# A one-core decode block: the rows of w_out loaded by other queues in other shares, the MLP in 8 pieces instead of 14, x loaded row by row

## The chip, the core and the metric

The kernel runs on one core of one Trainium2 chip. A core has a matrix engine (TensorE; PE in the profile, with its weight loads as PEld), a vector engine (VectorE, DVE), a scalar engine (ScalarE, ACT), a general engine (GpSimd, POOL) and a queue engine that mostly starts transfers (SyncE, SP). Sixteen DMA engines move data between the large memory (HBM) and the on-chip memory (SBUF), whose 128 partitions are called lanes here; matrix products land in PSUM. The metric is the time of one execution in device microseconds (us). Before the change it is 661.87 us, the median of 3 runs (661.77 to 662.01).

## What is computed

One token of each of four sequences (B = 4, D = 640) goes through attention over a cache of 4096 positions with 32 heads of 128, and, beside it, through a gated MLP; both are added to x. Cut to what matters:

```
xn = layernorm(x)                                            # x: 4 x 640
q  = xn @ wq                                                 # wq: 640 x 4096
o  = softmax(q . k_cache / sqrt(128)) . v_cache              # caches: 4 x 32 x 4096 x 128 each
z  = gelu(xn @ w_in)                                         # w_in: 640 x 1728
z1, z2 = z[:, :864], layernorm(z[:, 864:])
g  = w_sp * z2 + b_sp                                        # w_sp, b_sp: one number each
out = x + o @ wo + (z1 * g) @ w_out                          # wo: 4096 x 640, w_out: 864 x 640
```

All tensors are bf16. Nearly all bytes are in the two caches: 128 MiB each, of 282 MB read in all.

## The kernel before, in words

Work goes by units. A unit is 8 heads of one sequence, there are 16 of them (NU), and a unit's K and V are 8 MB each. In SBUF each lane holds 256 consecutive positions of one head, so a load of a unit is 128 lanes by 64 KB, each lane contiguous in HBM. A unit's K is worked on in four quarters (NK = 4); quarters live in a ring of seven places (`ring`). V has one place, `v_all`, of 64 KB a lane.

For each of the 64 quarters (the loop in the `manual_schedule` part) VectorE multiplies the quarter by q (`product`, L537) and adds its halves (`fold_half`, L543), TensorE sums the rest into PSUM (`sums`, L555), and VectorE reduces (`row_sums`, L569). Softmax follows once a unit (L578 to L607), then the products with V on TensorE (`weighted`, L631).

**Loads.** All large loads are issued by SyncE, in the order of the list `loads`. `pump()` goes down that list as long as the places that a load needs are free; a place is freed by the TensorE work that last read it. The list begins: the first quarter of K of unit 0, the second, `load_w` (w_in and those parts of w_out that go in one transfer), the other two quarters, `load_w_few` (the parts of w_out that go in several), K of unit 1, V of unit 0, K of unit 2 and so on. wq is issued ahead of all of them (L118). x, w_sp and b_sp are issued by ScalarE; w_sp and b_sp only inside the scheduled part, behind the first copy of q (L735, L736). A transfer signals its end on one of eight semaphores that transfers share in turn, so its issue can wait for an earlier transfer of the same semaphore.

**Places of the weights.** wq, w_in and the first 640 rows of w_out lie in `v_all` until the MLP is done, the other 224 rows of w_out in `p_buf`, which later holds the softmax weights `p_m`. V of unit 0 can therefore be loaded only once the MLP has read its weights.

**The MLP** (`gmlp`, a generator that the loop advances during the first two quarters) follows the rows of w_out: the hidden features are taken in pieces, and a piece is a set of features that lie on the lanes as the rows of w_out do. `W_OUT` lists parts as (lanes, rows a lane, transfers): 128 lanes of 5 rows, 128 lanes of 1 row, and 12 lanes of 8 rows in 4 transfers of 3 lanes. That makes NFC = 5 + 1 + 8 = 14 pieces. Each piece costs 10 products for z (two halves by five chunks of D, L404) and 2 for the output (L503); the small VectorE operations between work on all pieces at once (L414 to L500).

**The start.** GpSimd makes the identity and some constants; x is normalized on VectorE and ScalarE (L265 to L274), transposed on TensorE (L289), and multiplied by wq (L303) when that has landed.

**The end.** After V of unit 15 comes the last group of wo, in six transfers (L228, L231). The last products with it (L699), a copy (L823) and two small stores (L824, L825) end the program.

Of the kernel before, what the change touches and what calls it, by code (L numbers as in the profile page):

```python
# [10 lines left out]
BF16 = mybir.dt.bfloat16  # L11
# [6 lines left out]
def kernel(  # L18
# [40 lines left out]
    RW = 8  # L59
    QW = HC * Dh  # L60
    RING = 2 * NK - 1
    W_OUT = ((P, 5, 1), (P, 1, 1), (12, 8, 4))
    assert sum(n * r for n, r, _ in W_OUT) == Fh
    NFC = sum(r for _, r, _ in W_OUT)

    def up(n):
        return -(-n // 256) * 256

    PW = sum(up(r * D) for _, r, _ in W_OUT[1:])
    NOH = D // 2  # L70
    CB = 4
    NG = NR // CB
# [8 lines left out]
    const = ctx.enter_context(tc.tile_pool(name="const", bufs=1))  # L81
# [16 lines left out]

    ring = places.tile([P, RING, QW], BF16, name="k_ring")
    x_bf = ring[0:Bsz, 1, 0:D]  # L100
    nc.scalar.dma_start(out=x_bf, in_=A_x.flatten_outer_dims())
    v_all = places.tile([P, NK * QW], BF16, name="v_all")

    wq_sb = v_all[:, 0 : DC * HD].rearrange("p (c n) -> p c n", c=DC)
# [2 lines left out]

    at_v = up(DC * (HD + F))
    w_parts, f0, at_p = [], 0, 0
    for n, r, t in W_OUT:  # L110
        if f0 == 0:
            room = v_all[0:n, at_v : at_v + r * D]
        else:
            room = p_buf[0:n, at_p : at_p + r * D]
            at_p += up(r * D)
        w_parts.append((room.rearrange("p (k n) -> p k n", k=r), f0, n, r, t))
        f0 += n * r
    nc.sync.dma_start(out=wq_sb, in_=A_wq.rearrange("(p c) n -> p c n", c=DC))  # L118

    def load_part(part):  # L120
        w, f0, n, r, t = part
        rows = B_w_out[f0 : f0 + n * r].rearrange("(p k) n -> p k n", k=r)
        for l in range(t):
            nc.sync.dma_start(out=w[l:n:t], in_=rows[l:n:t])

    def load_w():
        nc.sync.dma_start(out=w_in_sb, in_=B_w_in.rearrange("(p c) n -> p c n", c=DC))
        for part in w_parts:
            if part[4] == 1:
                load_part(part)  # L130

    def load_w_few():
        for part in w_parts:
            if part[4] > 1:
                load_part(part)

    w_rows = [
        (w[:, i], f0 + i, n, r) for w, f0, n, r, _ in w_parts for i in range(r)
    ]
# [20 lines left out]
    def k_load(u, r0=0, r1=NK):  # L160
        at = k_at[u][r0:r1]

        def go():
            nc.sync.dma_start(
                out=ring[:, at[0] : at[0] + r1 - r0, :],
                in_=run_of(A_k_cache, u)[:, r0 * QW : r1 * QW].rearrange("p (r w) -> p r w", w=QW),
            )

        return go, at
# [22 lines left out]
    def wo_load(hg):  # L192
        return (lambda: load_wo(hg)), [WO_AT]

    loads = [k_load(0, 0, 1), k_load(0, 1, 2), (load_w, []), k_load(0, 2, 4), (load_w_few, []), k_load(1)]
    for u in range(NU - 4):
        loads += [v_load(u), k_load(u + 2)]
        if u % Bsz == Bsz - 1:
# [65 lines left out]
    for i in range(NSTAT):  # L264
# [5 lines left out]
        out=rstd[:], in_=mv[:, 1:2], func=ACT.Sqrt, bias=eps_tile[:Bsz], scale=1.0  # L270
# [4 lines left out]
        out=xn_bf,  # L275
# [4 lines left out]
        op1=ALU.mult,  # L280
    )

    wsp_bf = const.tile([1, 1], BF16)
    bsp_bf = const.tile([1, 1], BF16)

    xn_v = xn_bf.rearrange("b (p c) -> b c p", c=DC)
    xnT_ps = ps_m.tile([P, DC, Bsz], BF16, tag="m")
    for c in range(DC):
        nc.tensor.transpose(  # L289
            out=xnT_ps[:, c, :], in_=xn_v[:, c, :], identity=ident[:Bsz, :Bsz]  # L290
# [8 lines left out]
    for e in range(PAR):  # L299
        q_ps = ps_pv.tile([P, HG, Dh], FP32, tag="pv", name="q_ps")  # L300
        for c in range(DC):
            for k in range(NQ):
                nc.tensor.matmul(  # L303
                    out=q_ps[k * QD : (k + 1) * QD],
# [15 lines left out]
        out=hot[:].rearrange("p c h -> p (c h)"),  # L320
        in_=ident[:].rearrange("p (g m) -> p m g", m=QD),
# [23 lines left out]
    with nc.allow_low_precision("0 and 1"):  # L345
        nc.vector.tensor_reduce(
            out=own[:],
            in_=ident[:].rearrange("p (h l) -> p h l", h=HT),
# [5 lines left out]
        out=par[:], in_=own[:].rearrange("p (k e) -> p e k", e=PAR), axis=AX.X, op=ALU.add  # L354
# [3 lines left out]
        out=far[:],  # L358
# [13 lines left out]
    for half in range(2):  # L372
        nc.tensor.matmul(
            out=out_ps[OG * half : OG * half + OG, :],
# [16 lines left out]
    for n, r, _ in W_OUT:  # L391
        if by_lanes and by_lanes[-1][0] == n:
            by_lanes[-1] = (n, by_lanes[-1][1] + r)
        else:
            by_lanes.append((n, r))

    def gmlp():
        zz, gw, gt, gz = (gm[n] for n in ("zz", "gw", "gt", "gz"))
        zT = ps_pv.tile([P, 2, NFC, Bsz], FP32, tag="pv", name="zT")
        for t in range(2):  # L400
# [12 lines left out]
        for n, ks in by_lanes:  # L413
# [19 lines left out]

        s_ps = ps_m.tile([1, 2, NFC, Bsz], FP32, tag="m", name="ln_ps")
        nc.tensor.matmul(
# [79 lines left out]
    def stage_q(u):  # L515
        hg, b = divmod(u, Bsz)
        qb_ps = ps_m.tile([P, Dh], FP32, tag="m", name="qbc_ps")
        for e in range(PAR):
            nc.tensor.matmul(  # L519
                out=qb_ps[:],  # L520
                lhsT=of_row[:, e, b].rearrange("p k f l -> p (k f l)"),
                rhs=q_rows[e][:, hg, :],
                start=(e == 0),
                stop=(e == PAR - 1),
            )
        qbcs[u] = small.tile([P, Dh], BF16, name="qbc")
        nc.scalar.copy(out=qbcs[u][:], in_=qb_ps[:])  # L527
# [204 lines left out]
    E = mybir.EngineType  # L732
    with tc.manual_schedule(engines={E.PE, E.DVE, E.Activation, E.SP}):
        stage_q(0)
        nc.scalar.dma_start(out=wsp_bf[:], in_=B_w_sp[0:1, 0:1])  # L735
        nc.scalar.dma_start(out=bsp_bf[:], in_=B_b_sp[0:1].rearrange("(a b) -> a b", a=1))  # L736
        waiting = None
        mlp = gmlp()
        for n in range(NK * NU):
            u, i = divmod(n, NK)  # L740
# [33 lines left out]
            if n in turns:  # L774
                w = waiting = turns[n]
# [19 lines left out]
            out=den[:],  # L795
# [8 lines left out]
        u, b = NU - 1, Bsz - 1  # L804
# [51 lines left out]
```

## Time and profile before

| | before |
|---|---|
| median of 3 runs | 661.87 us (661.77 to 662.01) |
| the profiled execution: its own time | 662.09 us |
| the profiled execution: its span | 660.2 us |
| bytes read from HBM | 282.24 MB, 428 GB/s over the span |
| busy share: DVE, PE, PEld, ACT, POOL | 79%, 48%, 21%, 5%, 2% |
| DMA queue of SP (q1): packets, share of 16 engines | 8192, 99.1% |
| instruction loads (q8, q14): packets | 16 and 4 |
| DVE waiting for K to land (L537) | 87.9 us |

The span runs from the first to the last instruction of the profiled execution; what lies around it, 1.87 us, belongs to the execution's time as well. The page's DMA row gives the busy share of the sixteen DMA engines in 40 slices of the span, and the row below it what they moved. The trace also keeps each DMA packet with its queue, start, duration and bytes: a packet is one lane's contiguous piece, up to 64 KB, and each transfer ends on each DMA engine that serves it with a packet of 4 bytes that raises its semaphore. A packet doesn't name its DMA engine.

### The profile page before, as it was taken

Reading aid. Unit: us, or ns where it says so; the run is one execution under the profiler, and the core shown is the slowest. Engines: PE = TensorE matmul, PEld = TensorE weight load, DVE = VectorE, ACT = ScalarE, POOL = GpSimd, SP = SyncE. Lnnn points to the kernel's source line nnn. Section 1 sums busy time; section 2 is a strip of 40 time slices with the busy share of each in tenths; the row PEclk is TensorE's granted clock in tenths of the full one; section 3 lists DMA queues with packets and bytes.
Section 4 is the critical chain, followed back from the end, with each engine's and each line's share of the span. In section 5 each row is a group of like instructions: output and inputs, shape, how many; then the busy total and the mean of one; then the engine's idle time right before and its main releaser. Section 6 shows DMA issues by size and latency. Waiting matters only on the chain.

```text
span 660.2 us, 4777 instructions
## 1 busy us (share of the span) xinstructions
PE 317.0 (48%) x2083; PEld 136.3 (21%) x2083; DVE 522.6 (79%) x276; ACT 29.9 (5%) x73; POOL 10.1 (2%) x20
## 2 busy tenths in 40 slices
PE   0574372526427363452636336263452534737367
PEld 0231121212213121120212112121120211212124
DVE  1767978959597795969959598695969969999950
ACT  0020000000000000000000000000000000000000
POOL 2300000000000000000000000000000000000000
PEclk9757676766767676585767768676685867676785
DMA  9999999999999999999999999999999999999997
GB/s 369 433 461 434 417 441 434 433 437 438 421 445 426 437 430 441 437 422 433 434 441 441 418 437 441 430 441 421 434 441 437 426 421 445 422 427 436 449 409 284
DMA packets 8232, 282.55 MB, mean 428 GB/s; under 512 B 892, under 2 KB 2184, under 8 KB 2568
## 3 DMA queue, kind: packets, MB, share of 16 engines
q1 hardware_dynamic: 8192, 282.25, 99.1%
q8 instruction: 16, 0.26, 0.1%
q10 hardware_dynamic: 20, 0.01, 0.0%
q14 instruction: 4, 0.03, 0.0%
HBM read 282.24 MB, written 0.01 MB: 428 GB/s over the span
## 4 chain that ended last, share of the span: by engine, by line
DMA 62%; DVE 28%; PE 8%; issue 1%; ACT 0%; DVEq 0%
DMA k_ring<-in_A_k_cache_dram 53%; DVE k_ring L537 14%; DVE k_ring L543 7%; PE s_ps L555 6%; DMA v_all<-in_A_v_cache_dram 4%; DMA k_ring<-in_A_wo_dram 3%; DVE s_sb L569 3%; DMA v_all<-in_A_wq_dram 2%; DVE p_m L607 1%; DVE m L578 1%; PE q_ps L303 1%; PE pv L631 1%; PE out_ps L699 1%; DVE p_m L678 1%; DVE mf L580 1%
## 5 line engine op out<-in xcount | busy, mean ns | idle before, releaser
L537 DVE TENSOR_TENSOR k_ring<-k_ring,qbc 128x8192 bf16<-128x8192 bf16 x64 | 282.9, 4420 | 88.5 <-DMA k_ring<-in_A_k_cache_dram 87.9
L555 PE MATMUL s_ps<-k_ring,ident 128*128 128x512 bf16 x512 | 202.2, 566 | 313.8 <-DVE k_ring L543 313.7
L555 PEld LDWEIGHTS <-ident 128*128 128x128 bf16 x512 | 64.0, 130 | 430.0 <-issue 245.4
L543 DVE TENSOR_TENSOR k_ring<-k_ring 128x4096 bf16<-128x4096 bf16 x64 | 145.9, 2280 | 1.1
L631 PE MATMUL pv<-v_all,p_m 128*32 128x512 bf16 x960 | 62.5, 419 | 0.0
L569 DVE TENSOR_REDUCE s_sb<-s_ps 128x128 f32<-128x1024 f32 x32 | 39.0, 1218 | 3.7 <-PE s_ps L555 3.7
L607 DVE TENSOR_TENSOR p_m<-p_c,own 128x2048 bf16<-128x2048 bf16 x16 | 36.6, 2285 | 0.7 <-ACT p_c L596 0.7
L631 PEld LDWEIGHTS <-p_m 128*32 128x32 bf16 x992 | 26.6, 106 | 42.5 <-issue 23.3
L596 ACT ACTIVATE p_c<-s_sb,nm 128x256 bf16<-128x256 f32 x16 | 8.1, 508 | 342.9 <-DVE nm L588 342.9
L662 PEld LDWEIGHTS o_ps<-o_rows,pick 128*128 128x128 f32 x96 | 20.4, 294 | 4.3 <-issue 3.3
L662 PE MATMUL o_ps<-o_rows,pick 128*128 128x128 f32 x96 | 19.1, 367 | 0.0
L643 ACT COPY o_rows<-pv 128x512 f32<-128x512 f32 x16 | 9.4, 586 | 165.7 <-PE pv L631 165.7
L311 DVE TENSOR_SCALAR q_rows<-q_ps 128x512 bf16<-128x512 f32 x2 | 1.4, 692 | 12.8 <-PE q_ps L303 12.8
L817 DVE TENSOR_TENSOR o_n_last<-o_last,rden_all 128x32 bf16<-128x32 f32 x1 | 0.2, 192 | 12.2 <-PE o_last L809 12.2
L303 PE MATMUL q_ps<-v_all,xnT 128*32 128x512 bf16 x40 | 4.5, 630 | 9.3 <-DMA v_all<-in_A_wq_dram 9.3
L527 ACT CAST qbc<-qbc_ps 128x128 bf16<-128x128 f32 x16 | 4.3, 266 | 97.6 <-PE qbc_ps L519 97.6
L578 DVE TENSOR_REDUCE m<-s_sb 128x1 f32<-128x256 f32 x16 | 6.7, 420 | 0.5
L519 PE MATMUL qbc_ps<-q_rows,of_row 128*128 128x128 bf16 x32 | 6.0, 276 | 0.6 <-DVE q_rows L311 0.6
L519 PEld LDWEIGHTS <-of_row 128*128 128x128 bf16 x32 | 4.1, 132 | 8.1 <-issue 7.4
L716 PE MATMUL o_last<-hot,o_rows 128*128 128x8 f32 x32 | 4.9, 279 | 0.7 <-ACT o_rows L643 0.7
L716 PEld LDWEIGHTS o_last<-hot,o_rows 128*128 128x128 f32 x32 | 4.8, 226 | 1.8 <-ACT o_rows L643 1.6
L699 PE MATMUL out_ps<-k_ring,p_m 128*4 128x320 bf16 x48 | 4.0, 309 | 2.1 <-DVE p_m L691 2.1
(87 smaller groups left out, 81.4 us busy)
## 6 DMA issues: line engine op xcount, KB each, us to landing
k_ring<-in_A_k_cache_dram SPq DMA_DIRECT2D x5, 4096.0 KB, 27.2
v_all<-in_A_v_cache_dram SPq DMA_DIRECT2D x2, 4096.0 KB, 28.2
v_all<-in_A_wq_dram SPq DMA_DIRECT2D x1, 5120.0 KB, 15.4
k_ring<-in_A_k_cache_dram SPq DMA_DIRECT2D x2, 2048.0 KB
k_ring<-in_A_v_cache_dram SPq DMA_DIRECT2D x1, 4096.0 KB
k_ring<-in_A_wo_dram SPq DMA_DIRECT2D x3, 1280.0 KB, 20.6
v_all<-in_B_w_in_dram SPq DMA_DIRECT2D x1, 2160.0 KB
k_ring<-in_A_v_cache_dram SPq DMA_DIRECT2D x1, 2048.0 KB
```

The lines of the kernel that those rows point to most:

```text
L303: nc.tensor.matmul(out=q_ps[k * QD : (k + 1) * QD], lhsT=xnT[:, c, :], rhs=wq_v[:, c, k, e], start=(c == 0), stop=(c == DC - 1),)
L519: nc.tensor.matmul(out=qb_ps[:], lhsT=of_row[:, e, b].rearrange("p k f l -> p (k f l)"), rhs=q_rows[e][:, hg, :], start=(e == 0), stop=(e ...
L537: nc.vector.tensor_tensor(out=t, in0=t, in1=qbcs[u][:, None, :].to_broadcast([P, HC, Dh]), op=ALU.mult)
L543: nc.vector.tensor_tensor(out=t[:, :, 0:HD2], in0=t[:, :, 0:HD2], in1=t[:, :, HD2:Dh], op=ALU.add)
L555: nc.tensor.matmul(out=s, lhsT=ident[:], rhs=t[:, :, g * RW : (g + 1) * RW], start=(g == 0), stop=(g == m - 1),)
L569: nc.vector.tensor_reduce(out=scores[u][:].rearrange("p (r c) -> p r c", r=NK)[:, lo : hi + 1 : hi - lo], in_=sums_ps.pop(n // 2)[:], axis ...
L578: nc.vector.tensor_reduce(out=m1[:], in_=scores[u][:], axis=AX.X, op=ALU.max)
L607: nc.vector.tensor_tensor(out=p_m[:, u % 2], in0=p_c.pop(u)[:].rearrange("p (g c) -> p g c", c=CB)[:, :, :, None].to_broadcast([P, NG, CB, HT]
L631: nc.tensor.matmul(out=pvs[u][cg * QD : (cg + 1) * QD, :], lhsT=p_m[:, u % 2, g0 + n].rearrange("p c h -> p (c h)"), rhs=v_at[:, n * CB : ...
L662: nc.tensor.matmul(out=gr[hg][:], lhsT=pick[:, c, Bsz - 1 - b : P + Bsz - 1 - b], rhs=o[:, c, :], start=(b == 0 and c == 0), stop=(b == Bs ...
L699: nc.tensor.matmul(out=out_sum(half), lhsT=o, rhs=wo_sb[:, n, half * NOH : (half + 1) * NOH], start=False, stop=(hg == HG - 1 and n == HT ...
L716: nc.tensor.matmul(out=o_last[0][:, :, :, u % Bsz], lhsT=o[:, c, :], rhs=hot[:, c, :].rearrange("p (k e) -> p k e", e=PAR), start=(c == 0) ...
```

## The change

The last 224 rows of w_out are cut another way. Before, 128 rows went one to a lane in one transfer and 96 went 8 to a lane on 12 lanes, in four transfers of 3 lanes (every fourth lane), all by SyncE. Now 104 rows go one to a lane in three SyncE transfers of 95, 5 and 4 lanes, and 120 rows go two to a lane on 60 lanes, in two transfers issued by GpSimd, first the upper 14 lanes and then the lower 46. The two rows of such a lane are 60 rows apart in HBM, so they are two packets. The 640 rows of the first part are loaded as before.

The MLP then has 5 + 1 + 2 = 8 pieces, on 128, 104 and 60 lanes. The `load_w_few` entry of the list is gone: SyncE issues its three smaller transfers inside `load_w`, ahead of the last two quarters of K of unit 0, and GpSimd's two are the first instructions of its program after the start barrier. x is loaded in four transfers of one row; w_sp and b_sp are issued directly after them, at the start of ScalarE's program. The room in `p_buf` for these rows shrinks from 5888 to 2048 elements a lane, so that the buffer takes 5184, as many as the softmax weights need. By the instruction streams of the two programs, TensorE has 72 weight loads and 72 products fewer, VectorE one copy more.

```diff
-    W_OUT = ((P, 5, 1), (P, 1, 1), (12, 8, 4))
+    W_OUT = (
+        (P, 5, True, (("wide", 0, 128, 1),)),
+        (104, 1, True, (("wide", 0, 95, 1), ("wide", 95, 5, 1), ("wide", 100, 4, 1))),
+        (60, 2, False, (("pool", 46, 14, 1), ("pool", 0, 46, 1))),
+    )
...
-    nc.scalar.dma_start(out=x_bf, in_=A_x.flatten_outer_dims())
+    x_rows = A_x.flatten_outer_dims()
+    for b0, b1 in ((0, 1), (1, 2), (2, 3), (3, 4)):
+        nc.scalar.dma_start(out=x_bf[b0:b1], in_=x_rows[b0:b1])
+    wsp_bf = const.tile([1, 1], BF16)
+    bsp_bf = const.tile([1, 1], BF16)
+    nc.scalar.dma_start(out=wsp_bf[:], in_=B_w_sp[0:1, 0:1])
+    nc.scalar.dma_start(out=bsp_bf[:], in_=B_b_sp[0:1].rearrange("(a b) -> a b", a=1))
...
     def load_part(part):
-        w, f0, n, r, t = part
-        rows = B_w_out[f0 : f0 + n * r].rearrange("(p k) n -> p k n", k=r)
-        for l in range(t):
-            nc.sync.dma_start(out=w[l:n:t], in_=rows[l:n:t])
+        w, f0, n, r, near, cuts = part
+        rows = B_w_out[f0 : f0 + n * r].rearrange(
+            "(p k) n -> p k n" if near else "(k p) n -> p k n", k=r
+        )
+        for engine, l, m, step in cuts:
+            end = l + (m - 1) * step + 1
+            dma = nc.gpsimd if engine == "pool" else nc.sync
+            dma.dma_start(out=w[l:end:step], in_=rows[l:end:step])
...
-            if part[4] == 1:
-                load_part(part)
-
-    def load_w_few():
-        for part in w_parts:
-            if part[4] > 1:
-                load_part(part)
+            load_part(part)
...
-    loads = [k_load(0, 0, 1), k_load(0, 1, 2), (load_w, []), k_load(0, 2, 4), (load_w_few, []), k_load(1)]
+    loads = [k_load(0, 0, 1), k_load(0, 1, 2), (load_w, []), k_load(0, 2, 4), k_load(1)]
...
-        nc.scalar.dma_start(out=wsp_bf[:], in_=B_w_sp[0:1, 0:1])
-        nc.scalar.dma_start(out=bsp_bf[:], in_=B_b_sp[0:1].rearrange("(a b) -> a b", a=1))
```

More of the change, by code (lines that the diff above doesn't have):

```diff
@@ L61 @@
     RING = 2 * NK - 1
-    W_OUT = ((P, 5, 1), (P, 1, 1), (12, 8, 4))
-    assert sum(n * r for n, r, _ in W_OUT) == Fh
-    NFC = sum(r for _, r, _ in W_OUT)
+    W_OUT = (
[3 more added lines that the diff above has]
+    )
+    assert sum(n * r for n, r, _, _ in W_OUT) == Fh
+    NFC = sum(r for _, r, _, _ in W_OUT)
     def up(n):
         return -(-n // 256) * 256
-    PW = sum(up(r * D) for _, r, _ in W_OUT[1:])
+    PW = sum(up(r * D) for _, r, _, _ in W_OUT[1:])
     NOH = D // 2
@@ L109 @@
     w_parts, f0, at_p = [], 0, 0
-    for n, r, t in W_OUT:
+    for n, r, near, cuts in W_OUT:
         if f0 == 0:
@@ L115 @@
             at_p += up(r * D)
-        w_parts.append((room.rearrange("p (k n) -> p k n", k=r), f0, n, r, t))
+        w_parts.append((room.rearrange("p (k n) -> p k n", k=r), f0, n, r, near, cuts))
         f0 += n * r
@@ L128, in load_w @@
         for part in w_parts:
-            if part[4] == 1:
-                load_part(part)
-    def load_w_few():
-        for part in w_parts:
-            if part[4] > 1:
-                load_part(part)
+            load_part(part)
     w_rows = [
-        (w[:, i], f0 + i, n, r) for w, f0, n, r, _ in w_parts for i in range(r)
+        (w[:, i], f0 + i * (1 if near else n), n, r if near else 1)
+        for w, f0, n, r, near, _ in w_parts
+        for i in range(r)
     ]
@@ L281 @@
     )
-    wsp_bf = const.tile([1, 1], BF16)
-    bsp_bf = const.tile([1, 1], BF16)
     xn_v = xn_bf.rearrange("b (p c) -> b c p", c=DC)
@@ L390 @@
     by_lanes = []
-    for n, r, _ in W_OUT:
+    for n, r, _, _ in W_OUT:
         if by_lanes and by_lanes[-1][0] == n:
```

## The prediction, made before the changed kernel had run

> **What bounds the kernel now.** I read four views, in this order: the page's rows by slice, the table of windows at the end of the span, the timeline of SP's issues, and the DMA packets one by one. The page first:
>
> ```profile
> span 660.2 us, 4777 instructions
> ...
> DVE  1767978959597795969959598695969969999950
> ...
> DMA  9999999999999999999999999999999999999997
> ...
> q1 hardware_dynamic: 8192, 282.25, 99.1%
> q8 instruction: 16, 0.26, 0.1%
> ```
>
> The DMA engines are never idle; VectorE, the busiest compute engine, has gaps all along. So the bytes bound the time, and the question is which DMA engine ends last. The windows show that they don't end together (columns: window, its length, busy time of PE, PEld, DVE, ACT, POOL with counts, PE clock, DMA share, GB/s):
>
> ```profile
> 600.00:653.00 53.00, 34.24 (x338) 16.56 (x337) 36.92 (x22) 2.96 (x7) 0.00 (x0) 0.73 0.99 426
> 653.00:654.00 1.00, 0.40 (x15) 0.41 (x16) 0.00 (x0) 0.00 (x0) 0.00 (x0) 0.50 1.02 370
> 654.00:655.00 1.00, 0.72 (x12) 0.32 (x9) 0.19 (x1) 0.00 (x0) 0.00 (x0) 0.50 0.86 303
> 655.00:656.00 1.00, 0.87 (x6) 0.21 (x4) 0.00 (x0) 0.00 (x0) 0.00 (x0) 0.50 0.55 182
> 656.00:656.70 0.70, 0.59 (x6) 0.39 (x6) 0.00 (x0) 0.00 (x0) 0.00 (x0) 0.50 0.17 49
> ```
>
> The share falls from 0.99 to 0.17 over three microseconds: engines drop out from 653.4 us on, and the last stops at 656.63. Behind that lie only the last products, a copy and the store, as the end of the chain says:
>
> ```profile
> 634.09 21.98 DMA k_ring<-in_A_wo_dram
> 656.07 0.04 issue
> 656.11 1.29 PE out_ps L699 x8
> ...
> 657.43 0.42 ACT v_all L823
> ```
>
> Third, SP's issues, to see whether any transfer is issued too late to keep the engines busy:
>
> ```profile
> 0.73 0.39 SPq L118 DMA_DIRECT2D v_all<-in_A_wq_dram  x1
> ...
> 16.12 0.33 SPq L164 DMA_DIRECT2D k_ring<-in_A_k_cache_dram  x1
> 20.95 7.95 SPq L124 DMA_DIRECT2D p_m<-in_B_w_out_dram  x4
> 32.04 0.34 SPq L164 DMA_DIRECT2D k_ring<-in_A_k_cache_dram  x1
> 46.29 0.33 SPq L175 DMA_DIRECT2D v_all<-in_A_v_cache_dram  x1
> 75.45 0.33 SPq L164 DMA_DIRECT2D k_ring<-in_A_k_cache_dram  x1
> ```
>
> By the packets, the first bytes of these last three move at 41.44, 60.76 and 80.08: they are queued 9.4, 14.5 and 4.6 us ahead. Over the whole run a K load is never less than 2.8 us ahead.
>
> Last, the packets. On a busy engine the next packet starts 3 or 4 ns before the end of the one before it, so they can be laid end to end into sixteen chains. None of the sixteen waits for an issue after its start at 1.7 to 2.7 us. The only gaps over 20 ns belong to instruction loads. The sixteen of q8 go in turn to eight engines, two each; one costs its engine about 1.4 us (a gap of 0.86 to 0.95, and a packet of 2.95 instead of 2.42). The chains end:
>
> - eight engines with two instruction loads: 656.00, .02, .11, .13, .22, .30, .33 and 656.63
> - three that carried the 12 lanes of w_out (four packets of 10 KB, 0.387 us each, 1.55 in all): 654.96, 655.15, 655.45
> - five with neither: 653.43, 653.90, 654.20, 654.38, 654.98
>
> So the end is set by the engines that load instructions. Bytes taken off them count, bytes put on the other eight count only once these come last.
>
> **The change, part by part.**
>
> *SP's one-row transfer of 128 lanes goes.* It puts 8 rows on each engine, which took 0.42 us (its semaphore packets stand at 31.73 to 32.95, those of the transfer before at 31.32 to 32.53), 0.052 a row. All sixteen get 0.42 shorter.
>
> *The four 3-lane transfers go:* 1.55 off three engines that don't come last: nothing at the end.
>
> *SP's 95, 5 and 4 lanes.* No row shows these counts; the trace has 128 lanes as 16 equal shares, 4 lanes (x) as 4 and 3 as 3. Equal shares on at most 16 engines make 95 five times 19, 5 five times 1, and 4 four times 1. The three engines of the 3-lane transfers are then the likely first three: 21 rows x 0.052 = 1.09 us, in place of 0.42 + 1.55. The fourth and fifth gain 0.67. One engine of these two is likely among the five idle ones, since the fourth row of x preceded a chain that ended at 653.90: 654.6. If the fifth loads instructions it ends at 656.0 to 656.6 + 0.67, at most 657.3. The other bound is 95 rows on one engine, 4.9 us on 653.4: 657.9. I take the five, at no cost to the end.
>
> *GpSimd's 14 lanes of 2 rows.* Equal shares: 2 rows on each of 14 engines, 0.10 us. An engine that loads instructions then loses 0.42 and gains 0.10: **-0.31** for the end.
>
> *GpSimd's 46 lanes of 2 rows.* Equal shares are 2 x 23: two engines take 46 rows, 2.39 us, 1.97 over the 0.42 taken away. On two of the five idle engines that gives 655.4 to 656.9. Most of these pairs lie near or below 656.3, so I count nothing, and +0.3 as the far end. On engines that load instructions it is a rival. [...]
>
> *x in four transfers, w_sp and b_sp behind them.* x landed at 2.65, and the normalized, transposed x was ready at 7.13, 9 us before wq (first product at 16.15). If single rows go through one engine, each data and each semaphore packet takes turns with one wq packet, as w_sp's packets did with w_in's (25.96, 26.61, 27.25, 27.90, always one 0.64 us packet between). Eight of them need at most the first seven wq packets, 1.74 + 2.67 + 6 x 1.514 = 13.5 us; then 4.5 us of normalizing make 18.0, and q is 1.9 us late. The K load at 32.04 moves to about 34 of the 41.44 at which its bytes are due. The lower bound is no delay. Both cost nothing, since those 9.4 us cover them. Rows split finer over all engines would add some 8 packets of 9 to 20 ns to each: +0.1 at most.
>
> *SP's queue at the start.* Each issue now waits for a transfer sharing its semaphore: the second K quarter and w_in for rows of x, the w_out parts for rows of x, wq and w_sp, the last K quarters for b_sp. That ends by about 18 us instead of 16.12; their bytes are due at 31.74. Before, SP stood 7.95 us on the four small transfers waiting for w_sp and b_sp; that goes, but behind it the K load waits for its place (32.04) anyway: nothing.
>
> *MLP in 8 pieces.* 60 of 140 products and 12 of 28 go: 60 x 33 ns (4.61 us for 140) = 2.0 us, and 12 x 0.15 = 1.8. VectorE has one copy more (0.17) and shorter operations. The chain L404 to L503 gets about 4 us shorter, and V of unit 0 could be issued at 42 instead of 46.29; but its bytes are due at 60.76, so the cover of 14.5 us hides this gain, as it would hide a loss. For TensorE there are 142 instructions fewer, and the last of the sixteen instruction loads came at record 4164 of 4194: it should go. It was on an engine ending at 656.13, not the last: nothing.
>
> *GpSimd's issues* stand ahead of the identity (ready at 2.16, needed once x is normalized, and its constants by 20.5 at the latest). No row shows what they take. The nearest are SP's issues, 0.33 to 0.56 us each; up to 14 us for both is covered by wq, and some 8 us more by the 9.4.
>
> *GpSimd's rows on the lanes:* 46 packets taking turns with SP's are done after about as many SP packets, near 34 us; they are read at about 42. Nothing.
>
> **Sum.** 656.63 - 0.31 = 656.32 against the other seven, at most 656.02, and the two heavy engines near 656. The span becomes 659.9, the profiled execution 662.09 - 0.31 = 661.78. That execution lies 0.22 above the median of 661.87, so the forecast is **661.6 us**; its own range is 661.2 to 662.3 (an early or late first packet moves a chain by some 0.4, and +0.3 from above).
>
> **Rivals.**
>
> - *GpSimd's transfers are spread over all sixteen engines*, three lanes and one lane each: 8 rows again on the engines that load instructions. Then 661.9, no change.
> - *The two heavy shares hit engines that load instructions* (slower). Eight of the thirteen engines without a name do, so chance alone would favour it; against it, the eight are served in turn, and if they are neighbours, the ends of the row are more likely free. From 656.0 to 656.6 the end moves by 1.97, to 658.0 to 658.6: 663.2 to 663.9. It decides from 1.3 us of added time on.
> - *GpSimd's issues hold up the start.* If both take over about 22 us, the identity is late, the K load of 32.04 comes after 41.44, and every engine stands idle; at 25 us this gives some 3 us, 665. For it: a 1-element cast on GpSimd took 4.39 us. Against it: VectorE has nothing to do then. [...]
>
> **Chances.** Forecast 0.52, spread evenly 0.17, heavy shares in the wrong place 0.17, late start 0.05, other small losses of startup 0.06, and 0.03 for a gain beyond 1.3 us, for which seven engines would all have to end 1 us earlier. A measurement of this kernel can tell about 0.2%, 1.3 us, from no change. Forecast, spread and small losses are within it (0.75); slower is 0.22 and faster 0.03. The range takes in the forecast, the even spread and the heavy shares: 661.0 to 663.9.
>
> **What would show it.** Ends of the DMA engines between 655 and 656.4 instead of 653.4 to 656.6, so a shorter fall of the DMA share; 15 instruction loads; a new DMA queue with about 120 packets of 1280 bytes; q a little late and no idle DMA slice; V of unit 0 issued near 43. Wrong would be: DMA gaps before 60 us, or one pair of engines ending 2 us after the others.

## The result: half a per cent slower

The changed kernel takes 665.32 us (median of 9 executions, 664.13 to 670.38) against 661.87 (9 executions, 661.76 to 662.01): a ratio of **1.0058, 95% interval 1.0048 to 1.0068**. The forecast was 661.6, and the range ended at 663.9.

The profiled execution of this comparison took 670.38 us. From about 35 to 80 us its packets of 32 and 64 KB took 12% longer (2.714 us instead of 2.418 for 64 KB), on all sixteen engines, which the profile of another execution of the same kernel lacks; the readings here are therefore made on the profiled execution of the first run below, the same kernel again, at 665.47 us.

### The profile after

The page of that execution:

```profile
span 663.3 us, 4644 instructions
...
GB/s 351 411 443 435 431 436 443 424 431 439 432 431 435 432 435 443 420 435 435 440 431 439 420 435 436 431 436 443 435 428 435 435 428 443 410 432 443 445 406 253
...
q1 hardware_dynamic: 8142, 282.09, 98.9%
q8 instruction: 16, 0.26, 0.1%
q0 software_dynamic: 240, 0.16, 0.1%
```

The same row of the kernel before:

```profile
GB/s 369 433 461 434 417 441 434 433 437 438 421 445 426 437 430 441 437 422 433 434 441 441 418 437 441 430 441 421 434 441 437 426 421 445 422 427 436 449 409 284
```

The span is 3.1 us longer. The first two slices of the GB/s row show 351 and 411, where the kernel before has 369 and 433, and the last shows 253 instead of 284; the rest looks alike. So speed is lost in the first 35 us or so, and the end has a longer tail. The new queue q0 is GpSimd's; its 240 packets are not what I had expected of 120 rows (below). The instruction loads are still sixteen.

The windows say the same more sharply (columns as in the prediction: window, length, busy time of PE, PEld, DVE, ACT, POOL, PE clock, DMA share, GB/s). First the kernel before, then the changed one:

```profile
5.00:23.00 18.00, 5.25 (x47) 2.16 (x48) 3.19 (x6) 1.04 (x3) 0.41 (x3) 1.00 0.98 421
23.00:40.00 17.00, 8.66 (x153) 5.91 (x153) 14.36 (x13) 3.13 (x4) 6.10 (x2) 0.65 1.02 436
40.00:600.00 560.00, 265.10 (x1512) 109.99 (x1511) 466.27 (x229) 21.52 (x58) 0.00 (x0) 0.68 1.00 434
```

```profile
5.00:23.00 18.00, 4.75 (x47) 1.79 (x47) 3.20 (x11) 1.58 (x2) 2.43 (x11) 1.00 0.99 390
23.00:40.00 17.00, 8.48 (x96) 5.77 (x92) 14.61 (x9) 1.81 (x3) 0.00 (x0) 0.59 1.04 430
40.00:600.00 560.00, 259.73 (x1502) 106.53 (x1503) 466.01 (x235) 23.05 (x60) 0.00 (x0) 0.67 1.00 433
```

The last two columns are the lesson of this case. The DMA share is full in both kernels (0.98 and 0.99, then 1.02 and 1.04; above 1 because a packet counts whole in the window in which it starts), and yet the changed one moves 390 GB/s instead of 421 from 5 to 23 us, and 430 instead of 436 from 23 to 40. An engine that is busy all the time can still be slower, because its packets take longer. At the 434 GB/s of the long window, 31 x 18 + 6 x 17 GB/s x us are worth 1.5 us.

The packets show which ones. Those of 16 KB take 0.611 us each in the kernel before; in the changed one 149 of the 256 take over 0.64, and these start between 15.1 and 23.0 us. Those of 32 KB take 1.213; while SyncE's 104 rows go by, at 33.09 to 34.91 us, every one of the 21 beside them takes 1.32 or more (median 1.451, up to 1.62), and right behind them the median is 1.213 again. I add up, over SyncE's queue, how much longer each packet took than is usual for its size, and divide by the sixteen engines; call this the **lengthening**. The kernel before has 0.74 us of it, all in the first 20 us, where the first packets start up. The changed one has 1.90 in the first 20 us and 0.72 in the next 20: **1.88 us more, as a mean over the engines**.

The end, in windows of one microsecond of the changed kernel:

```profile
655.00:656.00 1.00, 0.66 (x19) 0.50 (x16) 0.00 (x0) 0.00 (x0) 0.00 (x0) 0.50 0.97 348
656.00:657.00 1.00, 0.39 (x14) 0.40 (x15) 0.00 (x0) 0.00 (x0) 0.00 (x0) 0.50 0.74 251
657.00:658.00 1.00, 0.72 (x12) 0.32 (x9) 0.19 (x1) 0.00 (x0) 0.00 (x0) 0.50 0.52 175
658.00:659.00 1.00, 0.88 (x6) 0.21 (x4) 0.00 (x0) 0.00 (x0) 0.00 (x0) 0.50 0.16 44
659.00:660.00 1.00, 0.95 (x8) 0.43 (x7) 0.00 (x0) 0.00 (x0) 0.00 (x0) 0.50 0.04 13
```

The last window still moves 13 GB/s with a share of 0.04, which is 0.6 of one engine's microsecond: **one engine alone** runs to 659.60. The other fifteen have ended by 658.13. The end of the chain of the same execution hangs on it:

```profile
637.04 21.96 DMA k_ring<-in_A_wo_dram
659.01 0.04 issue
659.05 1.34 PE out_ps L707 x8
...
660.41 0.42 ACT v_all L829
```

Against the 656.63 of the kernel before there are two losses: fifteen engines end up to 1.5 us later, and one ends another 1.47 us after them. (The chain names an arrival at 659.01 as the releaser; the last of the products behind it starts at 659.9, when the rows of 659.60 are there.)

Third, SyncE's issues in the changed kernel (start, time, queue, line, operation, tile, count):

```profile
0.74 0.39 SPq L128 DMA_DIRECT2D v_all<-in_A_wq_dram  x1
...
17.80 0.33 SPq L141 DMA_DIRECT2D v_all<-in_B_w_in_dram  x1
18.17 0.43 SPq L138 DMA_DIRECT2D v_all<-in_B_w_out_dram  x1
18.65 1.03 SPq L138 DMA_DIRECT2D p_m<-in_B_w_out_dram  x3
19.73 15.61 SPq L174 DMA_DIRECT2D k_ring<-in_A_k_cache_dram  x2
48.50 0.33 SPq L185 DMA_DIRECT2D v_all<-in_A_v_cache_dram  x1
77.82 0.33 SPq L174 DMA_DIRECT2D k_ring<-in_A_k_cache_dram  x1
```

The three transfers that replace the four small ones are issued in 1.03 us and nothing stands behind them; K of unit 1 goes out by 35.3, still 6 us before its bytes are due. No chain of packets has a gap for a late issue. The queue is as much ahead as the prediction counted on.

### The profile page after: what moved, and what is told of

Its sections match the earlier page's. It is cut to its first block, busy times and chain, and to the rows that moved or that the text cites. A ratio compares the mean times of both kernels' runs of the same rounds, so it can differ in the third digit from the quotient of the medians.

```text
span 668.2 us, 4644 instructions
## 1 busy us (share of the span) xinstructions
PE 308.0 (46%) x2011; PEld 130.5 (20%) x2011; DVE 522.4 (78%) x277; ACT 29.7 (4%) x73; POOL 6.2 (1%) x22
## 4 chain that ended last, share of the span: by engine, by line
DMA 62%; DVE 28%; PE 8%; issue 1%; ACT 0%; ACTq 0%; DVEq 0%
DMA k_ring<-in_A_k_cache_dram 53%; DVE k_ring L545 14%; DVE k_ring L551 7%; PE s_ps L563 6%; DMA v_all<-in_A_v_cache_dram 4%; DMA k_ring<-in_A_wo_dram 3%; DVE s_sb L577 3%; DMA k_ring<-in_A_x_dram 2%; DVE p_m L615 1%; DVE m L586 1%; PE q_ps L311 1%; PE out_ps L707 1%; DVE p_m L686 1%; PE pv L639 1%; DVE mf L588 1%
## 5 line engine op out<-in xcount | busy, mean ns | idle before, releaser
L639 PE MATMUL pv<-v_all,p_m 128*32 128x512 bf16 x960 | 61.1, 412 | 0.0
L670 PEld LDWEIGHTS o_ps<-o_rows,pick 128*128 128x128 f32 x96 | 17.3, 251 | 3.8 <-issue 2.7
L670 PE MATMUL o_ps<-o_rows,pick 128*128 128x128 f32 x96 | 16.1, 323 | 0.0
```

What stands on the lines that cost most here:

```text
L639: nc.tensor.matmul(out=pvs[u][cg * QD : (cg + 1) * QD, :], lhsT=p_m[:, u % 2, g0 + n].rearrange("p c h -> p (c h)"), rhs=v_at[:, n * CB : ...
L670: nc.tensor.matmul(out=gr[hg][:], lhsT=pick[:, c, Bsz - 1 - b : P + Bsz - 1 - b], rhs=o[:, c, :], start=(b == 0 and c == 0), stop=(b == Bs ...
```

## The experiments

Four theories stood at the start: x in single rows delays the start; SyncE's 95, 5 and 4 lanes lengthen the packets beside them; GpSimd's transfers do; and the heavy share of the 46 lanes lies on engines that load instructions (the rival of the prediction). "Lengthening" below is that of the run less the 0.74 of the kernel before. The kernel before took 661.95 to 662.0 us (medians) beside these runs.

### The same again, and x

The first run repeats the changed kernel.

> The changed kernel as it is, for a second profile. If the slow first 82 us of its profile (384 to 417 GB/s in five slices, 65536-byte packets of 2.71 us instead of 2.42) belong to the kernel, they come again and the time is near 670. If they were that execution's alone, the rate is back at 430 to 440 GB/s after the first two slices and the time is 665.3, with some 3.4 us over the kernel before still to be found.

It took 665.55 us, 1.0053 (1.0036 to 1.0069). The stretch of slow packets was not there; the rest is read above.

The second loads x in one transfer again:

```diff
-    for b0, b1 in ((0, 1), (1, 2), (2, 3), (3, 4)):
-        nc.scalar.dma_start(out=x_bf[b0:b1], in_=x_rows[b0:b1])
+    nc.scalar.dma_start(out=x_bf, in_=x_rows)
```

> x in one transfer again, the rest as changed. Late-start theory (x lands at 14.6 us instead of 2.65, w_in is issued at 17.7 instead of 2.83, and this costs the 3.4 us): x lands near 2.7 and the time falls to 662 or below. GpSimd theory (its two transfers slow the DMA engines): no change, 665.3. Ends theory (three engines end 1.2 us after the others because of their shares): no change at the end, 665.

665.23 us, 1.005 (1.0035 to 1.0065): as slow, within its interval. x in single rows is not the cause. In this run all sixteen chains of packets could be followed from start to end. At the landing of K of unit 1 the median engine stands at 63.36 us where the kernel before has 61.27, and at the end at 657.82 instead of 655.72: the 2.1 us are lost by then, and nothing is lost or gained afterwards. The two engines whose chains carry GpSimd's 5120-byte packets end their 16 KB packets at 27.7 and 29.0 us, 1.4 and 2.7 us behind the median engine, as 46 rows (2.39 us) would make them. **The first of the two has two instruction loads (gaps at 91.8 and 447.0 us) and ends last of all, at 659.52; the other has none and ends at 657.9.** So the heavy pair lies half on the engines that load instructions.

The third is the kernel before with x in four rows and w_sp and b_sp issued at the start, and nothing else:

```diff
-    nc.scalar.dma_start(out=x_bf, in_=A_x.flatten_outer_dims())
+    x_rows = A_x.flatten_outer_dims()
+    for b0, b1 in ((0, 1), (1, 2), (2, 3), (3, 4)):
+        nc.scalar.dma_start(out=x_bf[b0:b1], in_=x_rows[b0:b1])
...
+    nc.scalar.dma_start(out=wsp_bf[:], in_=B_w_sp[0:1, 0:1])
+    nc.scalar.dma_start(out=bsp_bf[:], in_=B_b_sp[0:1].rearrange("(a b) -> a b", a=1))
...
```

> The kernel before with only x in four transfers and w_sp and b_sp issued behind them. Late-start theory: 665. GpSimd theory and ends theory: 661.9, since the queue is 9.4 us ahead and nothing else has changed.

662.24 us, 1.0003 (0.9994 to 1.0012), no lengthening. x is out.

### SyncE's narrow transfers

GpSimd's two transfers are issued by SyncE instead:

```diff
-        (60, 2, False, (("pool", 46, 14, 1), ("pool", 0, 46, 1))),
+        (60, 2, False, (("wide", 46, 14, 1), ("wide", 0, 46, 1))),
```

> The transfers of 14 and 46 lanes issued by SyncE instead of GpSimd; their heavy shares then go to the first two engines. GpSimd theory: the packets of queue 0 are gone, no engine is held up at the start, and the time falls to about 662.2 (the first two engines now carry 67 to 71 rows, 3.2 us over the 653.5 at which they ended without extra rows, so 656.7). Late-start theory: 665.3, since x is still late.

664.06 us, 1.0031 (1.0019 to 1.0042). The windows of this run:

```profile
5.00:23.00 18.00, 5.48 (x48) 1.93 (x49) 3.50 (x12) 1.58 (x2) 0.84 (x5) 1.00 0.98 422
23.00:40.00 17.00, 8.10 (x91) 5.61 (x90) 14.67 (x11) 1.96 (x4) 0.00 (x0) 0.60 1.02 399
```

The loss moves with the transfers: 422 in the first window, as in the kernel before, and 399 instead of 436 in the second, where SyncE now sends all 224 rows (31.29 to 36.32 us). The 32 KB packets beside them take 1.665 in the median, up to 2.03. The lengthening is 1.35 us. So these narrow transfers lengthen the packets of other transfers, whichever of the two engines issues them. Less the 0.31 this explains one microsecond of the 2.07; the last engine ends at 658.18. By the forecast's equal shares, an estimate, SyncE's transfers of 95, 5, 4, 14 and 46 lanes put 21 + 2 + 46 rows on two engines, 3.6 us in place of 1.97: from 654.96 to 655.45 and with the lengthening that gives 657.9 to 658.4. Which engine it is was not followed.

Then the kernel before with its one-row transfer of 128 lanes cut into runs of lanes:

```diff
+        if (n, r) == (P, 1):
+            for l, e in ((0, 95), (95, 100), (100, 104), (104, P)):
+                nc.sync.dma_start(out=w[l:e], in_=rows[l:e])
+            return
```

> The kernel before, only its one-row transfer of 128 lanes cut into SyncE transfers of 95, 5, 4 and 24 lanes. Lane theory (in the 128-lane transfer each DMA engine writes lanes of its own, while a run of 19 neighbouring lanes on one engine goes where other engines write, so both are held up and everything beside it slows): the 32768-byte packets that move beside the row packets take 1.4 to 1.8 us instead of 1.21, as they did beside these transfers in the changed kernel, some 0.7 us an engine, and the time is 662.5. Shares theory (only the number of rows on an engine counts): these packets stay at 1.21, the engines that load instructions lose 6 rows, and the time is 661.6.

662.1 us, 1.0003 (0.9993 to 1.0012).

```profile
5.00:23.00 18.00, 5.19 (x47) 2.15 (x48) 3.07 (x6) 1.08 (x3) 0.45 (x3) 1.00 0.98 421
23.00:40.00 17.00, 8.54 (x152) 5.98 (x151) 14.21 (x12) 3.10 (x4) 6.07 (x2) 0.53 1.02 426
```

The same 104 rows, with a run of 24 lanes behind them, lower the second window from 436 to 426, and the 32 KB packets beside them take 1.43. The lengthening is 0.41 us. The time hardly moves all the same, because the cut also takes about 0.31 us of rows off the engines that come last: the last end is 656.56, before 656.63. I had expected 662.5.

### Is it the small packets, or GpSimd's queue?

The 12 lanes of w_out have their rows in 1280-byte packets instead of 10 KB ones, still every fourth lane:

```diff
-        rows = B_w_out[f0 : f0 + n * r].rearrange("(p k) n -> p k n", k=r)
+        rows = B_w_out[f0 : f0 + n * r].rearrange(
+            "(p k) n -> p k n" if t == 1 else "(k p) n -> p k n", k=r
+        )
...
```

> The kernel before, only the 8 rows of each of the 12 lanes lie 12 rows apart in HBM, so that the same three engines move 96 packets of 1280 bytes in place of 12 of 10240, every fourth lane as before. Lane theory: nothing beside them slows, the three engines need 1.66 instead of 1.55 us, and the time is 661.9. Small-packet theory (1280-byte packets on few engines slow all others): the packets beside them lengthen as in the changed kernel, some 0.6 us an engine, 662.5.

662.01 us, 1.0001 (0.9991 to 1.001); no lengthening, 32 KB packets at 1.213. Small packets by themselves cost nothing here.

The 128-lane transfer of one row goes to GpSimd:

```diff
-            nc.sync.dma_start(out=w[l:n:t], in_=rows[l:n:t])
+            dma = nc.gpsimd if (n, r) == (P, 1) else nc.sync
+            dma.dma_start(out=w[l:n:t], in_=rows[l:n:t])
```

> The kernel before, only its one-row transfer of 128 lanes issued by GpSimd. GpSimd theory (a transfer issued there slows the DMA engines by itself): 40960- and 16384-byte packets of the first 20 us are 5 to 14% longer, some 1.2 us an engine, and the time is 663. Lane theory: all engines write their own lanes, nothing lengthens, 661.9 to 662.1.

662.1 us, 1.0001 (0.9992 to 1.001).

```profile
5.00:23.00 18.00, 5.28 (x47) 2.23 (x48) 2.58 (x6) 0.92 (x3) 0.75 (x4) 1.00 0.99 424
23.00:40.00 17.00, 8.04 (x152) 5.79 (x151) 14.71 (x12) 2.94 (x4) 6.47 (x2) 0.67 1.01 433
```

424 and 433, the speeds of the kernel before, with more bytes from GpSimd's queue than the changed kernel sends there. Here a second queue beside SyncE's costs nothing. What is left, by elimination, is the shape: few lanes, side by side.

### GpSimd's lanes

The 60 lanes go in one transfer:

```diff
-        (60, 2, False, (("pool", 46, 14, 1), ("pool", 0, 46, 1))),
+        (60, 2, False, (("pool", 0, 60, 1),)),
```

> The changed kernel with GpSimd's 60 lanes in one transfer, so 4 lanes (8 rows) on each of 15 engines in place of 2 rows on fourteen and 46 on two. Heavy-share theory (one of the two engines with 46 rows also loads instructions and ends 1.2 us after the rest): no such engine is left, the end comes 0.9 to 1.2 us earlier, 664.3; what slows all engines in the first 40 us stays. Without it: 665.3.

> The changed kernel with GpSimd's 60 lanes in one transfer once more, for a profile without the stretch of 2.71 us packets that the first one had. Lane theory with heavy-share theory: the 16384-byte packets at 0.611 as in the kernel before, the 32768-byte packets beside the rows of 95, 5 and 4 lanes still 1.4 to 1.6, some 1.2 us an engine in all, and no engine more than 0.5 us after the others: a span of 661.

663.12 us, 1.0025 (1.001 to 1.0041), and 662.89 in the single execution of the second run, which is read here:

```profile
5.00:23.00 18.00, 4.64 (x47) 1.81 (x47) 3.13 (x11) 1.58 (x2) 1.15 (x6) 1.00 0.99 415
23.00:40.00 17.00, 8.66 (x100) 5.73 (x92) 14.46 (x9) 1.81 (x3) 0.00 (x0) 0.60 1.02 424
```

The first window recovers from 390 to 415. The lengthening falls to 0.80 us (0.34 and 0.46), and no engine is late: all have ended by 657.22. GpSimd's queue holds thirty packets of 5120 bytes, four rows each; in equal shares that is eight rows on each of fifteen engines.

The two transfers of the changed kernel, in the other order:

```diff
-        (60, 2, False, (("pool", 46, 14, 1), ("pool", 0, 46, 1))),
+        (60, 2, False, (("pool", 0, 46, 1), ("pool", 46, 14, 1))),
```

> The changed kernel with GpSimd's two transfers in the other order, 46 lanes first, so that the 46-row shares fall on another pair of engines. Heavy-share theory: if neither of the new pair loads instructions, the one late engine is gone and the end comes some 1.2 us earlier, 664.2; if one or both do, 665.3 again with one or two late engines. Lane theory alone: lengthening as before.

663.9 us in the median, 1.0029 of the kernel before. Two of the seven executions took 668.44 and 669.85, so the ratio of the comparison, which takes them in, is 1.0054 (1.0024 to 1.0084), and its interval does not part this order from the other; the other five lie at 663.64 to 663.95, where the changed kernel had 665.39 to 665.65 in the first run. What the order does is therefore read from the trace. The profiled execution took 663.85, and its end is this:

```profile
657.00:658.00 1.00, 0.89 (x8) 0.33 (x6) 0.00 (x0) 0.00 (x0) 0.00 (x0) 0.50 0.56 175
658.00:659.00 1.00, 0.84 (x6) 0.25 (x3) 0.00 (x0) 0.12 (x1) 0.00 (x0) 0.50 0.00 1
```

**The late engine is gone.** The last ends at 658.07; the window after 658 holds almost nothing, where the changed kernel had 44 and then 13 GB/s. The same bytes, packets and lanes, issued by the same engine: only which engines carry which rows has changed. At the landing of K of unit 1 two engines are 2.2 and 2.5 us behind the median, at 65.11 and 65.40 us. The end at 658.07 is 592.7 us after the later of them; in the kernel before, the earliest landing (60.76) and the earliest end (653.43) lie as far apart, and two instruction loads would add about 2.8 us, at the 1.4 us that one cost in the kernel before. So by these times neither of the two loads instructions now. The engines that do end at 657.4 to 657.87, before 656.0 to 656.63: 1.2 to 1.4 later, which is 1.61 of lengthening less the 0.31 of rows taken off them.

### Neighbouring lanes

If runs of neighbouring lanes are the point, the four 3-lane transfers of the kernel before should cost something when their lanes lie side by side:

```diff
-            nc.sync.dma_start(out=w[l:n:t], in_=rows[l:n:t])
+            m = n // t
+            nc.sync.dma_start(out=w[l * m : (l + 1) * m], in_=rows[l * m : (l + 1) * m])
```

> The kernel before, only that each of its four 3-lane transfers takes three neighbouring lanes (0 to 2, 3 to 5, 6 to 8, 9 to 11) in place of every fourth; same queue, same three engines, same packets of 10240 bytes. Lane theory: the three engines write the same few lanes at once, their packets take up to three times 0.385 us, their 1.55 us become 3 to 4.5, other packets for these lanes lengthen too, and since these engines end at 655.0 to 655.5 they become the last: 662.5 to 664. Shares theory: nothing changes, 661.9.

662.05 us, 1.0001 (0.9992 to 1.001). The expectation, 662.5 to 664, missed. The 10 KB packets of the last three transfers do take up to 0.816 us instead of 0.385, but that is 1.1 us over twelve packets, under 0.1 for an engine, and their neighbours show nothing.

The other test of it is a cut that should be cheap: 64 lanes with one row, and 20 lanes of 8 rows in transfers of five lanes, every fourth:

```diff
-    W_OUT = ((P, 5, 1), (P, 1, 1), (12, 8, 4))
+    W_OUT = ((P, 5, 1), (64, 1, 1), (20, 8, 4))
```

> The kernel before with the 224 rows as 64 lanes of one row and 20 lanes of 8, the latter in four transfers of 5 lanes, every fourth lane. The engines that load instructions then carry 4 of these rows in place of 8, five engines that don't carry 36. Lane theory and shares theory agree on -0.21 us from the 4 rows; the 64-lane transfer is partly on other engines' lanes, which takes up to 0.2 back under the lane theory: 661.7 to 661.9, against 661.7 without it.

662.04 us, 1.0 (0.9991 to 1.0009). It takes four rows, 0.21 us, off each of the engines that come last, and 0.21 us of lengthening beside the 64-lane rows (32 KB packets at 1.32) gives it back.

### GpSimd's 46 lanes alone

The kernel before with one more transfer by GpSimd ahead of everything, 46 lanes of two rows into a place that nobody reads, once with 32 bytes a row and once with whole rows:

```diff
+    extra_at = ring[0:46, 2, 0 : 2 * D].rearrange("p (k n) -> p k n", k=2)
+    extra_rows = B_w_out[744:836].rearrange("(k p) n -> p k n", k=2)
+    nc.gpsimd.dma_start(out=extra_at[:, :, 0:16], in_=extra_rows[:, :, 0:16])
```

> The kernel before with one more GpSimd transfer at the start, into lanes that nothing reads: the 46 lanes and 2 rows of the changed kernel, but only 32 bytes of each row. It keeps the two engines and whatever GpSimd writes for the fourteen others, and takes the data away. Filler theory (the 16-byte packets of GpSimd's queue, 154 = 11 x 14 in the changed kernel and 2 with 60 lanes in one transfer, take turns on the engines that carry no data and hold them up): about as many 16-byte packets, the 16384-byte packets beside them again near 0.69 us instead of 0.611, some 1 us an engine, 662.9. Data theory (rows on other engines' lanes do it): no lengthening, 662.0.

> The same extra transfer with whole rows, 118 KB more to read (0.27 us of all sixteen engines). Both theories: lengthening in the first 20 us as in the changed kernel, some 1 us an engine; and two engines with 2.4 us more work, one of which may end last: 663 to 664.5. Beside the run with 32 bytes a row it gives the data's part.

The small one: 662.31 us, 1.0006 (0.9997 to 1.0016), with 416 GB/s in the first window. One 40 KB packet on each engine, started between 7.1 and 8.3 us, takes 0.2 us longer there, and the lengthening is 0.26 us: neither the 1 us of the one theory nor the nothing of the other. The large one: 663.63 us, 1.0025 (1.0015 to 1.0034), with these windows:

```profile
5.00:23.00 18.00, 5.25 (x47) 2.17 (x48) 2.34 (x6) 0.51 (x2) 1.44 (x7) 1.00 0.98 401
23.00:40.00 17.00, 8.24 (x150) 5.90 (x149) 14.70 (x11) 2.21 (x4) 2.02 (x2) 0.57 1.02 435
```

401 instead of 421 in the first window, none in the second: this one transfer brings 0.95 us of lengthening as a mean over the engines, while its 118 KB are worth 0.27 us at 434 GB/s. The last engine ends at 658.11; those that load instructions would end by 657.6 with this lengthening, so it is likely one with 46 rows (argued, not followed).

I had meant to part two suspects with this pair. In the large one GpSimd's queue holds 24 packets with data (22 of four rows and two of two) and 154 packets of 16 bytes, by count eleven for each of the fourteen engines that carry none. In the small one the fillers came in one piece (14 packets of 184 bytes), so the pair does not tell the 16-byte packets from the rows. **That is left open.**

## Why the prediction was wrong

The loss of 3.5 us, part by part, with the runs that show it:

| part | us | shown by |
|---|---|---|
| rows taken off the engines that load instructions | -0.31 | forecast; ends of the run with the order swapped |
| lengthening beside GpSimd's 14 and 46 lanes | +1.16 | first 20 us of the changed kernel; the added 46 lanes alone gave 0.95 |
| lengthening beside SyncE's 95, 5 and 4 lanes | +0.72 | next 20 us of the changed kernel; 0.41 and 0.46 where GpSimd sent none, or one transfer of 60 lanes |
| 46 rows on one engine that loads instructions | +1.47 | 659.60 against 658.13; the swapped order, medians 665.55 to 663.9 |
| sum | +3.04 | measured: 663.3 - 660.2 = 3.1 of span, 3.45 by the medians of the comparison |

The other 0.3 us lie outside the span (2.2 us in the profiled execution, 1.9 before) and stay unexplained. The two rows of lengthening are parted by time alone. One at a time, the cut row gave 0.41 us and the added 46 lanes 0.95, 1.36 together; no run isolates the other 0.5 of the 1.88, which belongs to the 14 lanes or to both being there at once.

Point by point:

- **The bytes bound the time, and the DMA engine that ends last sets it: right.** So was the reading of who comes last, and the -0.31 for the engines that load instructions; it shows in the swapped order.
- **"SP's 95, 5 and 4 lanes ... at no cost to the end": the first step that failed.** The shares came as forecast (in the run with x in one transfer five engines without instruction loads carry 20 or 21 rows and end at 655.8 to 656.9). What was missing is what these rows do to the others: 0.4 to 0.7 us on all sixteen engines. I priced a row at 0.052 us, from the transfer of 128 lanes with 8 rows and 0.42 us on every engine, and put it on the engine that carries it alone. The trace of before had no narrow transfer of neighbouring lanes, and so no row for this; the term needed a bound above zero for the other engines, and I set none.
- **"GpSimd's 46 lanes ... I count nothing, and +0.3 as the far end": the second, and the larger.** Two engines did take 46 rows each (22 packets of four rows and two of two). But the transfers lengthen the other packets, by 1.2 us as a mean over the engines, and one of the two engines loads instructions.
- **The rival of the heavy shares came true in half.** One of the pair, not both. It was priced at 1.97 us from 656.0 to 656.6; with the lengthening of 1.88 that gives 659.9 to 660.5, and 659.60 was measured. Its 663.2 to 663.9 fell short because it had no term for the lengthening. I gave it 0.17 although eight of the thirteen unnamed engines load instructions; the argument against it, that the eight are neighbours and the ends of the row free, was a guess that no row bore out; no run shows which place in a row of engines the pair has.
- **The even spread over sixteen engines: wrong.** GpSimd's 38 packets of data are 22 of 5120 and 16 of 2560 bytes: 23 lanes on each of two engines and one lane on each of fourteen. The packets bear out the equal shares that the forecast counted with (two, fourteen and, with the 60 lanes in one transfer, fifteen engines with data). On which engines they fall, no row of before showed, and no run shows that the fourteen and the two make up the sixteen; the -0.31 needed two engines without instruction loads, and one of the two loads them in the changed kernel, neither with the order swapped. The shares tell nothing of the price for the others.
- **The late start: wrong.** GpSimd's two issues took 1.87 us together. The cast of 4.39 us that spoke for it ended at 33.08, with a product of 4.42 us on VectorE (33.04). The last packet of x ended at 14.18 us, forecast 13.5, and VectorE started on it at 14.82:

```profile
1.31 1.87 POOL L138 DMA_DIRECT2D p_m<-in_B_w_out_dram  x2 [0.87 <-POOLq L846]
```

- **x late, hidden: right, though the delay was larger.** The products for q began at 19.16 us in the profiled execution of the comparison, forecast 18.0; the 9.4 us of cover held, and x in rows alone costs 0.25 us at most by its median.
- **SyncE's queue: right at the end, with another wait.** I had w_in waiting for a row of x; it went out at 17.80, when wq had landed. K of unit 1 went out at about 35, forecast 34.
- **The MLP 4 us shorter, V of unit 0 issued near 43: wrong, and of no account.** It was issued at 48.50 (47.06 in the other execution), 46.29 before. The bytes are due 14 us later, so neither the gain nor the delay counts. Two things met: the MLP's first product starts 3.0 us later (34.95 instead of 31.96), because q is late, and the products that read `v_all`, for which V waits, are done 13.5 us after that instead of 14.3, so only 0.8 us shorter; the rest of the shortening lies in the products from `p_m` behind them.
- **Fifteen instruction loads: wrong.** Sixteen came with 142 instructions fewer on TensorE; the last moves from 658.6 us on, when only the late engine still has data.

The prediction's own signs of being wrong were gaps before 60 us, which there are none of, or a pair of engines 2 us behind the others; one engine was 1.5 us behind. That all packets might grow was not on the list.

**How far the cause is settled.** Shown: the lengthening comes with the narrow transfers and goes with them, whichever engine issues them; neither small packets nor a transfer from GpSimd on all lanes bring it by themselves; and the late engine comes from where the 46 rows fall. For GpSimd's part the 16-byte packets are not ruled out (above). Only conjectured is why neighbouring lanes do it: 128 lanes in sixteen equal shares are eight an engine, 95 lanes in five are nineteen, so an engine then writes lanes that in the loads beside it are another's, and the two might hold each other up. No trace shows which engine writes which lane. The runs with 128 lanes by GpSimd (424 and 433 GB/s against 421 and 436), with the cut row (0.41 us of lengthening) and with SyncE alone (1.35) fit this; the size does not follow from it (in sum over the engines 6.6 us for 6.7 us of rows in the cut row, 22 for 11.7 with SyncE alone), and the three neighbouring lanes, which I expected to show it, hardly did (1.1 us over twelve packets). So the runs bear out the effect for the wide runs of lanes tried here, and its mechanism is open.

## What to carry to other kernels

Where DMA engines are full throughout, price a transfer not only by the engine that carries it but by what it does to the packets beside it: compare GB/s at an equal DMA share, window by window (here 390 against 421 GB/s at 0.99 and 0.98). Keep transfers on all 128 lanes, or on every fourth lane as the small ones here (662.1 us with GpSimd's 128, 662.01 with small packets on every fourth); rows on runs of 46 to 95 neighbouring lanes cost the engines, in sum, as much time again as the rows themselves or more (6.6 us for 6.7 us of rows, 22 for 11.7), while three neighbouring lanes cost next to nothing (662.05 us). And where a narrow transfer gives two engines a large share, the order in which transfers are issued can decide whether they are engines that have other work, worth about 1.5 us here for 118 KB (medians of 665.55 and 663.9).

## What the hardware showed beyond that

- With GpSimd's 46-lane transfer come 154 packets of 16 bytes, by count eleven for each of the fourteen engines that carry none of its data, and its data packets of 5120 bytes gather four rows of 1280.
- These fillers move between 8.7 and 19.5 us in the changed kernel and the data packets between 5.5 and 22.6; the lengthened 16 KB packets start between 15.1 and 23.0. The 46 lanes alone give the same picture: fillers from 6.3 to 18.2, lengthened packets from 14.8 to 21.0.
- The stretch of packets that take 12% longer (64 KB in 2.714 us instead of 2.418) was seen twice, for some 45 us in the comparison (35 to 80 us) and for some 100 us with the 60 lanes in one transfer (37 to 138 us, 673.91 us). The page of the first has it in its third to fifth slice:

```profile
GB/s 351 417 401 384 389 436 428 439 432 439 432 432 428 440 432 428 436 432 439 432 440 428 437 428 425 439 435 440 432 429 435 435 419 437 424 434 433 451 406 256
```

From 35 to 82 us the lengthening is 4.9 us in it, which is 670.38 against 665.47. Single executions of 667.75 us (60 lanes in one transfer), 668.44 and 669.85 (the order swapped) were not profiled and may have had it too. What starts and ends the stretch is open.
